# Linear attention and a token/channel mixer on one core: v of the first head group by the plain queue, and another order for batch 1

## The chip, the core and the metric

The kernel runs on one core of a Trainium2 chip. Its engines are TensorE (PE in the profile; PEld is its weight load), VectorE (DVE), ScalarE (ACT), GpSimd (POOL) and SyncE (SP). Each engine works its own queue of instructions in order and they meet by semaphores. Transfers between the chip's memory (HBM) and the core's memory are issued on the queue of SP (hardware-made descriptors, no change of type) or of POOL (software-made descriptors, which can turn fp32 into bf16 under way), and all of them run on the same 16 DMA engines. Matmuls write to PSUM, which has eight banks here.

The metric is the device time of one execution in microseconds (us). A run's span, by the hardware profiler, is from the first instruction to the last; the time is a little longer.

## The reference

Eight batches, eight heads, 576 positions, head size 64; the attention output of one batch is a matrix of 576 x 512, which then goes through a mixer.

```python
phi = lambda x: np.where(x > 0, x, np.exp(x) - 1.0) + 1.0
q_p, k_p = phi(q), phi(k)
kv  = einsum('bhsd,bhse->bhde', k_p, v)
z   = sum(k_p, axis=2)
x   = einsum('bhsd,bhde->bhse', q_p, kv) / (einsum('bhsd,bhd->bhs', q_p, z) + 1e-6)
x   = x as (batch, 576, 512)
u   = x + (relu(x^T @ w_tok1) @ w_tok2)^T      # w_tok1 576 x 256, w_tok2 256 x 576
out = u + relu(u @ w_ch1) @ w_ch2              # w_ch1 512 x 1536, w_ch2 1536 x 512
```

All inputs and the output are fp32; matmuls are in bf16 with fp32 sums.

## The kernel before

The order of all instructions is written by hand; nothing is scheduled by a planner. Each batch's 576 positions are cut into four tiles of 128 (`R = 4`) and a tail of 64; two batches share the tail's 128 rows. The heads of a batch are handled in two groups of four (`c` or `g` = 0, 1).

The steps of a batch, by the names in the code:

- `phi`: e = exp(x) on ScalarE (L125), y = max(x + 1, 1) on VectorE (L131), min(e, y) on VectorE (L139), into `kp` or `qp`. `phi_exp`, `phi_add`, `phi_end` are these three parts; `fe`, `fa`, `fm` place them one by one for batch 1.
- `vcast`: v from fp32 to bf16 (L150), into `vs`, which has a column of ones behind each head's 64 columns.
- `kv`: 36 small matmuls kp^T @ vs (L168); the column of ones gives the sum of kp. Two ScalarE copies (L174) put the result into `kvbd`.
- `qtr`: nine transposes of qp on TensorE (L179), copied out to `qT` (L186). From batch 2 on it is a DMA transpose (`qtr_dma`).
- `nd`: numerator and denominator, qT @ kvbd (L209), then on VectorE den + eps (L218), reciprocal (L220) and the product into x (L221).
- `mm1`, `mm2`: the token mixer (L247 / L258 and L270 / L306, L309); u = x + h. For batch 1 these run in halves of the columns (`mm1_half`, `mm2_half`); the tail is `mm2(1, [R])`, which takes a bank of the pool of four banks (`ps_big`), while for the other batches it lies in the pool of two double banks (`ps_sm`).
- `utr`: u transposed to uT (L325, copy L328), later by DMA.
- `mm3`: uT @ w_ch1, twelve blocks `mc` of four 512-column matmuls (L493), relu to bf16 on ScalarE (L500) or, for two of them, VectorE (L497).
- `mm4`: cr @ w_ch2 (L519); `mm4_end` adds u on VectorE (L536) and sends the rows out.

Steady state: for each batch, a list `big` of blocks of TensorE work (mm3 and mm4) is run through, and a list `fill` says behind which block each step of the next batch stands (`run`). An entry `at(8, vcast, 1, 0)` stands behind block 8. Since every engine's queue is in order, the place in this list is the place in each queue that the step touches.

For batch 0 and 1 the list has 24 blocks: 0 to 2 the second halves of mm3's first three `mc`, 3 to 11 mm3 (`mc` 3 to 11), 12 to 21 `m4_0(kc)`, in which all four row tiles of mm4 get the share of one `kc`, and 22 and 23 `m4_end` (the last two `kc` for row tiles 0, 1 and then 2, 3). So from block 12 to the end mm4's four sums `held[0]` to `held[3]` occupy all four banks of `ps_big`, until `mm4_end(0, t)` has read them.

The start, batch 0, is written out by itself (lines 583 to 706): `e_first`, `r_first`, `p_first` are phi's parts; `kv_first`, `ksum_mm`, `den_mm`, `num_mm` and so on are the steps above in another cut. Here v is loaded by POOL's queue as bf16 into `v0` (`load_v0`, L113, a part of the memory of `cr[1]`), which has no column of ones; so the sum of kp is made by nine extra matmuls (`ksum_mm`, L357) and copied by `ksum_put` (L362). `warm` issues fp32 matmuls on zeros whose result nobody reads.

A gate is a wait put by hand in front of a transfer (`after(ins, other)`): it is issued only when `other` has landed. Before the change q of group 1 waits for k of group 0 (`k_in`), the second v load for the first (`v_in`), batch 1's k of group 0 for the first quarter of w_ch1 (`c_in[0]`) and k of group 1 for its last (`c_in[3]`), the second quarter of w_ch2 for v of batch 1, group 0, and batch 2's q for the second quarter of w_ch2 (`c2_in[1]`). A gated load holds all that stands behind it in its queue.

Of the kernel before, what the change touches and what calls it, by code (L numbers as in the profile page):

```python
# [18 lines left out]
def kernel(  # L19
# [20 lines left out]
    nc = tc.nc  # L40

    B, H, S, D = q.shape
# [3 lines left out]
    R = 4  # L46
# [10 lines left out]
    D1 = D + 1  # L57
# [7 lines left out]
    def const(name, shape, dt=BF16):  # L65
        return consts.tile(shape, dt, name=name, tag=name)
# [36 lines left out]
    def after(ins, other):  # L103
        if other is not None:
            tc.add_manual_dep(ins.ins, other.ins.name, sync_dep, reason="order of transfers")
        return ins

    def load(nm, n, c, gate=None):
        src_ = src[nm][n].rearrange("(j a) (p t) d -> (a p) j (t d)", a=2, t=T)
        js = slice(2 * c, 2 * c + 2)  # L110
        return after(nc.sync.dma_start(out=raw[nm, n % 2][:, js], in_=src_[:, js]), gate)

    def load_v0(c, gate=None):  # L113
        src_ = v[0].rearrange("(j a) (p t) d -> (a p) j (t d)", a=2, t=T)
# [13 lines left out]
    def phi_add(nm, n, j0, nj):  # L128
        f = raw[nm, n % 2][:, j0:j0 + nj].rearrange("p j f -> p (j f)")
        y = work.tile([128, 2 * TD], BF16, name="y", tag="y")[:, :nj * TD]  # L130
        nc.vector.tensor_scalar(out=y, in0=f, scalar1=1.0, scalar2=1.0, op0=ALU.add, op1=ALU.max)  # L131
        for j in range(nj):
            live["y", nm, j0 + j] = y[:, j * TD:]

    def phi_end(nm, n, j0, nj):
        c, i = divmod(j0, 2)
        dst = (kp if nm == "k" else qp)[:, c, :, i:i + nj]
        e, y = live["e", nm, j0], live["y", nm, j0][:, :nj * TD]
        nc.vector.tensor_tensor(  # L139
            out=dst.transpose([0, 2, 1, 3]), in0=e.rearrange("p (i t d) -> p i t d", i=nj, t=T),  # L140
            in1=y.rearrange("p (i t d) -> p i t d", i=nj, t=T), op=ALU.min)
# [6 lines left out]
    def vcast(n, c, copy=nc.scalar.copy):  # L148
        js = slice(2 * c, 2 * c + 2)
        copy(out=vs[:, js, :, 0:D],  # L150
             in_=raw["v", n % 2][:, js].rearrange("p j (t d) -> p j t d", t=T))

    def bank():
        return ps_big.tile([128, 512], FP32, name="bank", tag="big")
# [195 lines left out]

    def qput_first(c, h, put):
        qtr_put(0, c, TS[h], live["qtr", c][h], put, qT[c])

    def ksum_mm(c):
        ps = live["g", c][:, 0:2]
        for t in range(T):
            nc.tensor.matmul(out=ps, lhsT=kp[:, c, t].rearrange("p i d -> p (i d)"),  # L357
                             rhs=ones, start=(t == 0), stop=(t == T - 1))

    def ksum_put(c, copy):  # L360
        for i in range(2):
            copy(out=kvbd[0][half[i], c, :, (i + 1) * D1 - 1], in_=live["g", c][half[i], 0:2])  # L362

    def kv_first(c):

        ps = live["kv", c]
        for t in range(T):
            for a, i in QUARTERS:
                nc.tensor.matmul(out=ps[a][half[i], i * D:(i + 1) * D], lhsT=kp[half[a], c, t, i],
                                 rhs=v0[half[a], 2 * c + i, t],  # L370
                                 start=(t == 0), stop=(t == T - 1))

    def kv_put(c, copy):
        for i in range(2):
            for a in range(2) if c else [slice(0, 2)]:
                copy(out=kvbd[0][half[i], c, a, i * D1:(i + 1) * D1 - 1],
                     in_=live["kv", c][a][half[i], i * D:(i + 1) * D] if c else
                     live["kv2"][half[i], :, i * D:(i + 1) * D])

    def q_cols(r, a, c):  # L380
        t0 = D * (T * (2 * a + c) + 2 * r)
# [203 lines left out]
    nc.vector.memset(zeros, 0.0)  # L585
    nc.vector.memset(one, 0.0)
    nc.scalar.activation(out=one, in_=one, func=AF.Exp)
    k_in = load("k", 0, 0)
    load("q", 0, 0)
    make_identity(nc, identity)  # L590
    v_in = load_v0(0)
    load("q", 0, 1, k_in)
    load("k", 0, 1)
    nc.vector.memset(ones, 0.0)
    for a in range(2):
        nc.vector.memset(ones[half[a], a:a + 1], 1.0)
# [9 lines left out]
    NB = 4  # L606
# [18 lines left out]
    dve, act, pool = nc.vector.tensor_copy, nc.scalar.copy, nc.gpsimd.tensor_copy  # L625
    c_in = [load_wc1(i) for i in range(3)]
# [1 line left out]
        w2_put(kt, t0, t1, pool)  # L628
    c_in.append(load_wc1(3))
    nc.gpsimd.dma_start(out=w1t[half[1], 1, :], in_=w1r[:, 2 * R])  # L630
    c2_in = [load_wc2(0)]

    w_ = bank()
    live["g", 0] = bank()
    live["qtr", 0] = [bank16(), bank16()]
    t_ = sm_tile()
    live["kv2"] = t_[:, :, 0:2 * D]
    live["kv", 0] = [t_[:, a, 0:2 * D] for a in range(2)]
    live["last", 0] = t_[:, 0, 256:256 + HG * D]
    t_ = sm_tile().rearrange("p b (r c) -> p b r c", r=2)  # L640
    live["full", 0] = [t_[:, i] for i in range(2)]
    e_first("k", 0)
    r_first("k", 0)
    warm(w_, 3)
    p_first("k", 0)
    ksum_mm(0)
    e_first("q", 0)
    r_first("q", 0)
    warm(w_, 1, 256)
    kv_first(0)  # L650
    ksum_put(0, act)
    kv_put(0, act)
    p_first("q", 0)
    qtr_first(0)
    qput_first(0, 0, dve)
    qput_first(0, 1, act)
    warm(w_, 1, 256)
    e_first("q", 1)
    r_first("q", 1)
    den_mm(0)  # L660
    num_mm(0)
    den_first(0)
    warm(w_, 1, 256)
    live["qtr", 1] = [bank16(), bank16()]
    live["g", 1] = bank()
    p_first("q", 1)
    e_first("k", 1)
    r_first("k", 1)
    qtr_first(1)
    warm(live["g", 1], 1, 256)  # L670
    p_first("k", 1)
# [35 lines left out]

    for c in range(2):
        for nm in "kqv":
            landed[nm + "1", c] = load(nm, 1, c, c_in[3 * c] if nm == "k" else None)  # L710
    c2_in += [after(load_wc2(i), landed["v1", 0] if i == 1 else None) for i in range(1, NB)]
    for nm in "qkv":
        for c in range(2):
            load(nm, 2, c, c2_in[1] if nm == "q" and c == 0 else None)
# [50 lines left out]
    def fe(s, nm, c):  # L765
        fill.append((s, lambda: phi_exp(nm, 1, 2 * c, 2)))

    def fa(s, nm, c):
        fill.append((s, lambda: phi_add(nm, 1, 2 * c, 2)))

    def fm(s, nm, c):
        fill.append((s, lambda: phi_end(nm, 1, 2 * c, 2)))

    def at(s, fn, *args):
        fill.append((s, lambda: fn(*args)))

    fe(2, "k", 0)
    fa(2, "k", 0)
    fm(3, "k", 0)
    fe(5, "q", 0)  # L780
    fa(5, "q", 0)
    fm(6, "q", 0)
    at(8, qtr, 1, 0, dve)
    at(8, vcast, 1, 0)
    at(10, kv, 1, [0])
    at(11, nd, 1, 0, [0, 1])
    fe(11, "k", 1)
    fa(11, "k", 1)
    at(12, nd, 1, 0, [2, 3])
    fe(12, "q", 1)  # L790
    at(13, nd, 1, 0, [R])
    fm(13, "k", 1)
    fa(13, "q", 1)
    fm(14, "q", 1)
    at(14, vcast, 1, 1)
    at(15, mm1_half, 1, 0)
    at(16, kv, 1, [1])
    at(17, qtr, 1, 1, act)
    at(18, mm2_half, 1, 0)
    at(18, nd, 1, 1, [0, 1])  # L800
    at(19, nd, 1, 1, [2, 3])
    at(20, nd, 1, 1, [R])
    at(20, phi, "q", 2, 0)
    at(20, phi, "q", 2, 1)
    at(21, utr, 1, [0])
    at(21, mm1_half, 1, 1)
    at(22, qtr_dma, 2)
    at(22, load_all, 3, "qkv")
    at(22, mm4_end, 0, 0)
    at(22, mm4_end, 0, 1)  # L810
    at(22, mm2_half, 1, 1)
    at(23, mm2, 1, [R])
    at(23, mm4_end, 0, 2)
    at(23, utr, 1, [1])
    at(23, mm4_end, 0, 3)
    run(big, sorted(fill, key=lambda e: e[0]))

# [69 lines left out]
```

## Time and profile before

| | |
|---|---|
| time, median of 13 runs | 265.39 us (264.68 to 266.55) |
| the profiled execution | 265.11 us, span 263.3 us |
| first matmul of mm1_first (L430) | 16.63 us |
| first matmul of mm3 (L493) | 23.26 us |
| block 3 (mm3, mc 3) | 27.19 us |
| block 12 (m4_0(0), L519) | 36.21 us, with the first nd ahead of it |
| batch 1's mm3 begins | 54.95 us |
| landings: k_raw, q_raw of group 0 | 4.55 and 5.95 us |
| landings: v0 first and second part | 8.2 and 14.7 us |
| landings: q_raw, k_raw of group 1 | 10.46 and 11.9 us |
| landing of wc1's first and last quarter | 19.88 and 29.19 us |
| landing of wc2's first and second quarter | 32.9 and 39.28 us |

The times of instructions are starts on the span's clock. The landings follow from the time of issue and the time to landing of each transfer, or from the end of the wait of the instruction that needed it. From some 57 us to the end TensorE has no hole to speak of: what it does there is the same work in each pair of batches.

### The profile page before, as it was taken

The page shows a single profiled execution, that of the slowest core. Times are in us where ns is not written, and L with a number is a line of the kernel's source. Part 1 is how long each engine was busy: PE and PEld are TensorE (multiplying, and loading weights), DVE is VectorE, ACT ScalarE, POOL GpSimd, SP SyncE. Part 2 cuts the span into 40 slices and gives each one's busy share as a digit, 9 for nine tenths or more (in the row PEclk, how much of TensorE's full clock was granted, in tenths as well). Part 3 has the DMA queues.
Part 4 walks back from the last instruction along what each step waited for, and adds up shares of the span by engine and source line. Part 5 has one row for each costly group of instructions (what it writes and reads, how often), then busy time and mean ns, then how long its engine had stood idle before and what let it go on. Part 6 is the DMA issues. An engine that isn't in the chain of part 4 may idle for free.

```text
span 263.3 us, 5086 instructions
## 1 busy us (share of the span) xinstructions
PE 254.2 (97%) x2080; PEld 132.8 (50%) x2080; DVE 143.8 (55%) x285; ACT 133.9 (51%) x212; POOL 32.1 (12%) x57
## 2 busy tenths in 40 slices
PE   7789999999999999999999999999999999999994
PEld 2565456644744454445554554445554554444642
DVE  4675753976867385848564285828564272520122
ACT  4663794659662358425871368325870363027300
POOL 3752120030001300030001300030001300000000
PEclk9979999999999999999999999999999999999999
DMA  7999999879829990699999980761064500740043
GB/s 210 254 190 271 293 280 290 317 133 316 341 65 162 313 369 4 137 231 364 406 319 218 329 338 1 164 146 42 0 137 114 123 0 2 149 110 0 2 99 100
DMA packets 50087, 48.34 MB, mean 184 GB/s; under 512 B 30288, under 2 KB 35536, under 8 KB 50064
## 3 DMA queue, kind: packets, MB, share of 16 engines
q1 hardware_dynamic: 41904, 35.53, 44.6%
q0 software_dynamic: 7440, 11.44, 21.4%
q10 hardware_dynamic: 720, 1.05, 1.2%
q8 instruction: 16, 0.26, 0.4%
q14 instruction: 7, 0.06, 0.1%
HBM read 35.85 MB, written 9.44 MB: 172 GB/s over the span
## 4 chain that ended last, share of the span: by engine, by line
PE 86%; DMA 6%; DVE 5%; ACT 1%; issue 1%; DVEq 0%
PE c_ps L493 32%; PE h_ps L519 30%; PE a_ps L247 5%; PE c_ps L507 4%; PE h_ps L270 4%; PE nd_ps L209 3%; DMA uT<-u 2%; DMA q_raw<-in_q_dram 2%; PE kv_ps L168 2%; DMA k_raw<-in_k_dram 1%; PE bank L430 1%; PE h_ps L556 1%; DVE y L131 1%; DVE qp L139 1%; DVE o_sb L536 1%; DVE x L221 1%
## 5 line engine op out<-in xcount | busy, mean ns | idle before, releaser
L500 ACT ACTIVATE cr<-c_ps 128x512 bf16<-128x512 f32 x92 | 54.0, 599 | 78.3 <-PE c_ps L493 78.3
L493 PE MATMUL c_ps<-uT,wc 128*128 128x512 bf16 x384 | 91.9, 379 | 0.3 <-DMA uT<-u 0.2
L519 PE MATMUL h_ps<-wc,cr 128*128 128x512 bf16 x372 | 84.9, 379 | 0.0
L519 PEld LDWEIGHTS <-cr 128*128 128x128 bf16 x372 | 35.6, 98 | 41.0 <-issue 1.2
L493 PEld LDWEIGHTS <-wc 128*128 128x128 bf16 x384 | 35.5, 98 | 36.8 <-issue 2.2
L536 DVE TENSOR_TENSOR o_sb<-h_ps,u 128x512 f32<-128x512 f32 x31 | 21.1, 689 | 24.2 <-PE h_ps L519 24.1
L541 POOL DMA_DIRECT2D out_dram<-o_sb x24 | 14.5, 607 | 152.1 <-DVE o_sb L536 152.1
L221 DVE TENSOR_TENSOR x<-nd_ps,den 128x512 bf16<-128x512 f32 (+1 forms) x42 | 25.3, 603 | 1.4
L125 ACT ACTIVATE e<-k_raw 128x1152 bf16<-128x1152 f32 x16 | 18.7, 1169 | 2.6 <-DMA k_raw<-in_k_dram 2.6
L139 DVE TENSOR_TENSOR qp<-e,y 128x1152 bf16<-128x1152 bf16 x16 | 12.1, 759 | 14.0 <-ACT e L125 13.3
L282 DVE TENSOR_TENSOR u<-h_ps,x 128x1024 bf16<-128x1024 f32 x12 | 14.7, 1222 | 9.2 <-PE h_ps L270 9.2
L125 ACT ACTIVATE e<-q_raw 128x1152 bf16<-128x1152 f32 x16 | 18.4, 1159 | 1.0 <-DMA q_raw<-in_q_dram 0.8
L218 DVE TENSOR_SCALAR den<-nd_ps 128x8 f32<-128x8 f32 (+1 forms) x42 | 6.9, 163 | 21.1 <-PE nd_ps L209 20.5
L139 DVE TENSOR_TENSOR kp<-e,y 128x1152 bf16<-128x1152 bf16 x16 | 12.1, 758 | 8.2 <-ACT e L125 7.3
L209 PEld LDWEIGHTS <-qT 128*128 128x128 bf16 x140 | 11.4, 98 | 9.4 <-issue 0.4
L209 PE MATMUL nd_ps<-kvbd,qT 128*128 128x130 bf16 x140 | 15.1, 223 | 0.2 <-ACT u L312 0.2
L150 ACT CAST vs<-v_raw 128x1152 bf16<-128x1152 f32 x13 | 15.0, 1156 | 0.0
L131 DVE TENSOR_SCALAR y<-k_raw 128x1152 bf16<-128x1152 f32 x16 | 12.4, 772 | 2.0 <-DMA k_raw<-in_k_dram 1.9
L546 DVE TENSOR_TENSOR o_sb<-h_ps,ut 128x512 f32<-128x512 f32 x4 | 2.8, 692 | 19.1 <-PE h_ps L519 19.1
L131 DVE TENSOR_SCALAR y<-q_raw 128x1152 bf16<-128x1152 f32 x16 | 12.0, 753 | 0.8 <-DMA q_raw<-in_q_dram 0.8
L247 PE MATMUL a_ps<-x,w 128*128 128x512 bf16 x48 | 12.3, 379 | 0.0
L270 PE MATMUL h_ps<-ar,w2p 128*128 128x512 bf16 x48 | 12.3, 379 | 0.0
(107 smaller groups left out, 206.4 us busy)
## 6 DMA issues: line engine op xcount, KB each, us to landing
k_raw<-in_k_dram SPq DMA_DIRECT2D x16, 576.0 KB, 9.2
q_raw<-in_q_dram SPq DMA_DIRECT2D x16, 576.0 KB, 6.6
v_raw<-in_v_dram SPq DMA_DIRECT2D x14, 576.0 KB, 11.4
out_dram<-o_sb POOLq DMA_DIRECT2D x24, 256.0 KB, 5.1
wc<-in_moe_w_ch_dram POOLq DMA_DIRECT2D x8, 384.0 KB, 9.1
out_dram<-o_sb SPq DMA_DIRECT2D x9, 128.0 KB, 2.3
out_dram<-o_sb ACTq DMA_DIRECT2D x7, 128.0 KB, 2.6
out_dram<-o_sb POOLq DMA_DIRECT2D x6, 128.0 KB, 5.7
```

The costliest lines, as they stand in the source:

```text
L125: nc.scalar.activation(out=e, in_=f, func=AF.Exp)
L131: nc.vector.tensor_scalar(out=y, in0=f, scalar1=1.0, scalar2=1.0, op0=ALU.add, op1=ALU.max)
L139: nc.vector.tensor_tensor(out=dst.transpose([0, 2, 1, 3]), in0=e.rearrange("p (i t d) -> p i t d", i=nj, t=T), in1=y.rearrange("p (i t d) ...
L150: copy(out=vs[:, js, :, 0:D], in_=raw["v", n % 2][:, js].rearrange("p j (t d) -> p j t d", t=T))
L209: nc.tensor.matmul(out=o[:, a], lhsT=qT[b][:, t0:t0 + 128], rhs=kvbd[b][:, c, a], start=True, stop=True)
L221: nc.vector.tensor_tensor(out=x[b][:, rs[0]:rs[0] + m, HG * D * g:HG * D * (g + 1)].rearrange("p r (h d) -> p r h d", h=HG), in0=v_[:, :, ...
L247: nc.tensor.matmul(out=ps[:, mt], lhsT=w1t[:, b, ms] if r == R else w1[:, r, ms], rhs=x[b][:, r, :], start=(r == 0), stop=(r == R))
L270: nc.tensor.matmul(out=ps[:, i], lhsT=w2v(kt, r, b), rhs=ar[b][:, kt, :], start=(kt == 0), stop=(kt == NT - 1 and not add))
L493: nc.tensor.matmul(out=ps, lhsT=wc1[:, kj, 128 * mc:128 * mc + 128], rhs=uT[b][:, :, kj], start=(kj == 0), stop=(kj == NDM - 1))
L500: nc.scalar.activation(out=cr[b][:, mc, :], in_=ps, func=AF.Relu)
L519: nc.tensor.matmul(out=ps, lhsT=crt[:, kc, :] if t == 8 else cr[b][:, kc, 128 * r:128 * r + 128], rhs=wc2[:, kc, :], start=(kc == 0), stop ...
L536: nc.vector.tensor_tensor(out=o, in0=ps, in1=u[b][:, r, :], op=ALU.add)
```

## The change

Five things change.

1. v of batch 0, group 0 is loaded as fp32 on SP's queue into `raw["v", 0]`, as k and q are, in the order k, q, v, q of group 1, k of group 1. No gate stands between them. VectorE casts it to bf16 (`vcast(0, 0, dve)`), and `kv_first(0)` uses `vs` with its column of ones, so group 0 needs no `ksum_mm`, `ksum_put`. Group 1's v is loaded by POOL as before, gated on group 0's v.
2. In the start, group 0's order becomes: phi of k and of q, transposes of q, cast of v, one of the two copies of the transposes, kv, its copies, the other copy. The warm matmuls are placed otherwise (four at the beginning in place of three, two behind `den_first(0)`, none ahead of kv). In group 1 phi's last part for q stands behind the first two parts for k.
3. Batch 1's six loads go out behind one another on SP's queue; only the first has a gate.
4. The first quarter of w_ch2 waits for q of batch 1, group 0; the second for k of batch 1, group 1.
5. Batch 1's steps, and those of batch 2's q, stand at other places among the 24 blocks.

```diff
     def kv_first(c):
-        ps = live["kv", c]
+        m = D if c else D1
         for t in range(T):
             for a, i in QUARTERS:
-                nc.tensor.matmul(out=ps[a][half[i], i * D:(i + 1) * D], lhsT=kp[half[a], c, t, i],
-                                 rhs=v0[half[a], 2 * c + i, t],
+                nc.tensor.matmul(out=live["kv", c][a][half[i], i * m:(i + 1) * m],
+                                 lhsT=kp[half[a], c, t, i],
+                                 rhs=(v0 if c else vs)[half[a], 2 * c + i, t],
...
-    k_in = load("k", 0, 0)
+    load("k", 0, 0)
     load("q", 0, 0)
+    v_in = load("v", 0, 0)
+    load("q", 0, 1)
+    load("k", 0, 1)
     make_identity(nc, identity)
-    v_in = load_v0(0)
-    load("q", 0, 1, k_in)
-    load("k", 0, 1)
...
-    c2_in = [load_wc2(0)]
+    c2_in = []
...
-    warm(w_, 3)
+    warm(w_, 4)
     p_first("k", 0)
-    ksum_mm(0)
     e_first("q", 0)
     r_first("q", 0)
-    warm(w_, 1, 256)
-    kv_first(0)
-    ksum_put(0, act)
-    kv_put(0, act)
     p_first("q", 0)
     qtr_first(0)
+    vcast(0, 0, dve)
+    qput_first(0, 1, act)
+    kv_first(0)
+    kv_put(0, act)
     qput_first(0, 0, dve)
-    qput_first(0, 1, act)
...
-    warm(w_, 1, 256)
+    warm(w_, 2, 256)
...
-    p_first("q", 1)
     e_first("k", 1)
     r_first("k", 1)
+    p_first("q", 1)
...
-            landed[nm + "1", c] = load(nm, 1, c, c_in[3 * c] if nm == "k" else None)
-    c2_in += [after(load_wc2(i), landed["v1", 0] if i == 1 else None) for i in range(1, NB)]
+            landed[nm, c] = load(nm, 1, c, c_in[0] if nm == "k" and c == 0 else None)
+    c2_in += [after(load_wc2(i), {0: landed["q", 0], 1: landed["k", 1]}.get(i)) for i in range(NB)]
```

The places in the list `fill`, behind which block each step stands:

| step | before | after |
|---|---|---|
| k, group 0: exp and add, then min | 2, 3 | 5, 6 |
| q, group 0: exp and add, then min | 5, 6 | 8, 9 |
| cast of v, transposes of q, group 0 | 8, 8 | 10, 11 |
| kv, group 0 | 10 | 11 |
| nd, group 0 (rows 0-1, 2-3, tail) | 11, 12, 13 | 12, 13, 14 |
| k, group 1: add, exp, min | 11, 11, 13 | 11, 12, 14 |
| q, group 1: exp, add, min | 12, 13, 14 | 13, 14, 14 |
| cast of v, group 1 | 14 | 14 |
| mm1_half, group 0's columns | 15 | 14 |
| kv, group 1 | 16 | 14 |
| mm2_half, group 0's columns | 18 | 15 |
| transposes of q, group 1 | 17 | 16 |
| utr, first half | 21 | 16 |
| nd, group 1 | 18, 19, 20 | 17, 18, 19 |
| phi of batch 2's q, groups 0 and 1 | 20, 20, ahead of mm1_half | 20 (behind mm1_half), 21 (behind mm2_half) |
| mm1_half, group 1's columns | 21 | 20 |
| mm2_half, group 1's columns | 22 | 21 |
| mm4_end of row tiles 0 and 1 | 22, ahead of mm2_half | 22 |
| utr, second half | 23 | 22 |
| mm2(1, [R]) | 23 | 22 |

More of the change, by code (lines that the diff above doesn't have):

```diff
@@ L374, in kv_put @@
         for i in range(2):
-            for a in range(2) if c else [slice(0, 2)]:
+            if c == 0:
+                at = slice(i * D1, (i + 1) * D1)
+                copy(out=kvbd[0][half[i], 0, :, at], in_=live["kv2"][half[i], :, at])
+            for a in range(2 * c):
                 copy(out=kvbd[0][half[i], c, a, i * D1:(i + 1) * D1 - 1],
-                     in_=live["kv", c][a][half[i], i * D:(i + 1) * D] if c else
-                     live["kv2"][half[i], :, i * D:(i + 1) * D])
+                     in_=live["kv", c][a][half[i], i * D:(i + 1) * D])
     def q_cols(r, a, c):
@@ L636 @@
     t_ = sm_tile()
-    live["kv2"] = t_[:, :, 0:2 * D]
-    live["kv", 0] = [t_[:, a, 0:2 * D] for a in range(2)]
+    live["kv2"] = t_[:, :, 0:2 * D1]
+    live["kv", 0] = [t_[:, a, 0:2 * D1] for a in range(2)]
     live["last", 0] = t_[:, 0, 256:256 + HG * D]
@@ L775, in at @@
         fill.append((s, lambda: fn(*args)))
[L777 to L787, printed above, removed]
-    fa(11, "k", 1)
[L789 to L793, printed above, removed]
+    fe(5, "k", 0)
+    fa(5, "k", 0)
+    fm(6, "k", 0)
+    fe(8, "q", 0)
+    fa(8, "q", 0)
+    fm(9, "q", 0)
+    at(10, vcast, 1, 0)
+    at(11, qtr, 1, 0, dve)
+    at(11, kv, 1, [0])
+    fa(11, "k", 1)
+    fe(12, "k", 1)
+    at(12, nd, 1, 0, [0, 1])
+    at(13, nd, 1, 0, [2, 3])
+    fe(13, "q", 1)
+    at(14, nd, 1, 0, [R])
+    fm(14, "k", 1)
+    fa(14, "q", 1)
     fm(14, "q", 1)
     at(14, vcast, 1, 1)
[L796 to L802, printed above, removed]
+    at(14, mm1_half, 1, 0)
+    at(14, kv, 1, [1])
+    at(15, mm2_half, 1, 0)
+    at(16, qtr, 1, 1, act)
+    at(16, utr, 1, [0])
+    at(17, nd, 1, 1, [0, 1])
+    at(18, nd, 1, 1, [2, 3])
+    at(19, nd, 1, 1, [R])
+    at(20, mm1_half, 1, 1)
     at(20, phi, "q", 2, 0)
-    at(20, phi, "q", 2, 1)
-    at(21, utr, 1, [0])
-    at(21, mm1_half, 1, 1)
+    at(21, mm2_half, 1, 1)
+    at(21, phi, "q", 2, 1)
+    at(22, mm4_end, 0, 0)
+    at(22, mm4_end, 0, 1)
     at(22, qtr_dma, 2)
     at(22, load_all, 3, "qkv")
[L809 to L812, printed above, removed]
+    at(22, utr, 1, [1])
+    at(22, mm2, 1, [R])
     at(23, mm4_end, 0, 2)
-    at(23, utr, 1, [1])
     at(23, mm4_end, 0, 3)
```

## The prediction

> **What bounds the kernel now.** I read the page first, then busy time by stretches, the chain of waits, the timeline by engine, and the DMA queues in single stretches.
>
> ```profile
> span 263.3 us, 5086 instructions
> PE 254.2 (97%) x2080; PEld 132.8 (50%) x2080; DVE 143.8 (55%) x285; ACT 133.9 (51%) x212; POOL 32.1 (12%) x57
> ```
>
> TensorE is busy for 97% of the span. No matmul of it is removed after the first 16 us (the diff only moves them), so the change acts in two ways: through when the dense stretch of TensorE begins and at what clock, and through new holes in it. The busy time by stretches (columns: stretch in us, its length, each engine's busy time and instructions, granted clock, DMA share, GB/s):
>
> ```profile
> 9.50:12.90 3.40, 2.25 (x32) 1.57 (x31) 2.49 (x6) 2.61 (x3) 3.40 (x6) 1.00 1.05 199
> 12.90:16.30 3.40, 2.40 (x69) 1.78 (x67) 2.87 (x7) 2.49 (x12) 1.55 (x2) 1.00 1.27 179
> 16.30:19.70 3.40, 3.40 (x22) 2.53 (x19) 2.24 (x4) 1.69 (x6) 1.98 (x4) 0.50 1.29 198
> 45.00:56.50 11.50, 11.11 (x85) 6.99 (x83) 9.94 (x20) 6.35 (x8) 1.24 (x2) 1.00 0.73 256
> ```
>
> The sparse start lasts until 16.3; then TensorE is full but has half its clock for 3.4 us; from 45 to 56.5 VectorE is the tight second engine (9.94 of 11.5). The chain of waits in order of time (start, length, what) shows how the start ends:
>
> ```profile
> 13.52 0.77 DVE kp L139
> 14.73 0.52 PE bank L369 x36
> 15.27 0.31 ACT kvbd L376 x2
> 15.86 0.97 PE bank L397 x10
> 16.83 3.65 PE bank L430 x20
> ```
>
> From the timeline (start, length, engine, line, what), the places where batch 1's steps stand today:
>
> ```profile
> 33.01 1.15 ACT L150 CAST vs<-v_raw 128x1152 bf16<-128x1152 f32 x1
> 34.75 0.48 PE L168 MATMUL kv_ps<-vs,kp 64*64 64x65 bf16 x36
> 46.44 2.25 ACT L125 ACTIVATE e<-q_raw 128x1152 bf16<-128x1152 f32 x2 [0.21 <-issue]
> 51.20 0.60 ACT L260 ACTIVATE ar<-a_ps 128x512 bf16<-128x512 f32 x1
> 52.66 1.28 DVE L536 TENSOR_TENSOR o_sb<-h_ps,u 128x512 f32<-128x512 f32 x2
> ```
>
> The cast ends 0.6 us ahead of its reader, and batch 2's exponentials are done long before the relu of mm1's second half. Last, the queues from 32.1 to 35 us (packets, MB, share), in which three wc2 loads had been issued on POOL's queue:
>
> ```profile
> q1 hardware_dynamic: 535, 1.16, 103.5%
> q0 software_dynamic: 8, 0.01, 1.4%
> ```
>
> POOL's queue moves nothing while SP's is full.
>
> **The start.** SP's queue alone moved 0.97 MB from 2.3 to 4.9 us, 0.37 MB/us. Five loads of 0.59 MB behind one another then land at about 4.55 (k, as today), 5.9, 7.5 (v), 9.0 (q1) and 10.5 (k1), against 4.55, 5.95, 8.25 (v0), 10.46 and 11.9. Group 0 by rows: qp 7.30 + 0.76 = 8.05 as today; v's cast, 0.75 (the one L150 on VectorE, at 62.4), 8.8; 36 matmuls of kv 0.48, 9.3; two ScalarE copies 0.27 each (L174), 9.9; den_mm 0.6, 10.5; den_first 0.5, 11.0; then on VectorE y of k1 0.76, qp 0.8, kp 0.8, so kp ends at 13.35, against 14.28. The transposes of q1 still end at 13.2. Behind them ScalarE has L186 0.59, two L419 0.53, ksum_put 0.32 and kv_put 0.65, in all 15.3, against 15.82. But v0's second load, on POOL behind v's landing, gets no engine until SP's queue is empty, at about 10.4; today it began to move after 10 too and landed at 14.7 (8.50 + 6.2). I take 14.4: kv of group 1 then ends at 14.9, kv_put at 15.6, and mm1 starts **0.3 earlier**. The weights behind it gain the same 0.3. Bounds: 0 (v's chain as long as today's) and 1.5 (k1's landing, 11.9 to 10.4). Dropping group 0's ksum (nine matmuls 0.38, two ScalarE copies 0.32) is worth nothing: it ran while TensorE waited 0.75 for v0. The fourth warm matmul lies before qp at 8.05; without that cover it costs 0.85 (5.11 / 6). The 256-column ones moved lie in waits.
>
> **The clock.** mm1_first took 3.65 us for 20 matmuls; at full clock ten of that form take 1.09 (L258), so 2.18: 1.47 is lost to the drop. The stretch ahead of the drop had 2.40 of 3.40 busy, the one ahead of that 2.25 without a drop; what differs is that the first holds 36 small and nine two-column matmuls. After the change the same stretch gains some 0.3 us of mm1 and the number of 128-column matmuls that today fall after 16.3, and the warm ones lie closer together: I take the drop to be gone. Then w2's copies on POOL (17.72 - 0.3 + 1.93 = 19.3) are late for mm2_first's second part, due at 16.3 + 2.2 + 0.44 = 18.95: 0.35 back. **-1.1**; bounds 0 and -1.47.
>
> The Trainium skill speaks differently ("TensorE: Matmul & The Clock Gate", Part 1): half rate comes after an idle window of about 3.4 us, so there should be no drop before or after. The row has one behind a stretch that is 70% busy; by the rule the sum would lack this gain, by the row it has it.
>
> **wc2's first quarter.** It no longer goes out at 20.86 but waits on POOL for q(1,0), which lands at 20.29 - 0.3 + 8.4 = 28.4. By then SP's queue also holds v and the second groups (no gate now): 6 x 0.59 = 3.5 MB, of which 1.2 are moved by 27.3 (58% beside the wc1 quarters, 1.09 MB in 22 to 27); the other 2.3 take 6 us, to 33.2. Today's wc2 load issued at 32.09 landed 7.0 to 7.2 later, at 39.28, some 3.6 after SP's queue had emptied at 35.7: so 36.8. The other bound is 28.4 + 7.0 = 35.4, and far out the longest wc row, 12.0: 40.4. I take 36.1, between the first two. Block 12 (m4_0(0)) wants it: today blocks 3 to 11 start at 27.19; the new start is 25.8, and block 12 is due 9.5 later (below), at 35.3. **+0.8**; bounds 0 and 1.5. The second quarter follows 2 us later, at 38.1 to 38.8, due after block 14: 25.8 + 15 = 40.8, so nothing. POOL has nothing else queued there until the first output.
>
> The skill ("DMA: Bandwidth & Descriptors", Queues, rings and completion order) has each engine go round the queues packet by packet. By that wc2's quarter would move from 29 on and land near 35.2; the two queue rows above show 8 packets against 535. By the rule the wait falls away, by the row it stands.
>
> **Batch 1's order** (zero is the start of block 3; a block of four takes 0.86). Four places, all from the order in which the new instructions stand:
> - ScalarE has e of k at 3.2, e of q at 5.8 (after block 8's relu), two relus of 0.5, the cast at 7.9, done at 9.05. TensorE is through block 11 and the nine transposes at 8.3, and kv waits: **+0.7**. Today's cast stood two blocks ahead of kv.
> - mm1_half(1, 0) stands right behind the last num matmul. Its bank is that of the nd before it, whose three VectorE steps (0.17, 0.20, 0.69, start 0.44 behind) end 1.6 after its first matmul, TensorE 1.2 after: 0.4; then the tail's x another 0.33. **+0.75**.
> - The exponentials of batch 2's q now stand behind mm1_half(1, 1) and its relu. From that matmul's end: relu 0.75, e 1.05, qp 0.8, then u (L314) 0.7, y 0.85, qp 0.7, o_sb 0.7: 5.4 us until bank held[0] is free. mm2(1, [R]) takes that bank (today after block 23, now before it). TensorE has two blocks, mm2_half 1.09 and eight transposes 0.45 until then, 3.3, and waits 0.35 within them for u: **+2.1**. Its cover would be VectorE idle before; it is idle for 2 us then, but its head waits for e.
> - Today's own holes go: 0.39 idle in 45 to 56.5, and three gaps each hide 0.16 of pipelined ends: **-0.9**.
> A further 0.1 for qtr's ScalarE copies ahead of nd. Together +2.75; bounds +1.3 (the middle two halved) and +3.6 (nothing of today's holes goes). Later loads (q of 2 behind wc2's second quarter) come 1 us earlier, batch 3's 2 to 3 us later, with ten blocks until used.
>
> **Sum.** -0.3 - 1.1 + 0.8 + 2.75 = +2.15 on a span of 263.3: 265.4. The profiled run took 265.11, 0.28 under the median, 1.8 outside its span. Median 265.39 + 2.2 = **267.6**; own range 266.4 to 268.8.
>
> **Rivals.**
> - The clock drop stays (the sparse stretch 12.9 to 16.3 is still mostly small matmuls, and full rate was kept with 2.25 busy, lost with 2.40). Block 12 is due at 36.4, so wc2's wait goes too: -0.3 + 2.75 = +2.45, 267.8.
> - The start gives all: k1's 1.5 and the whole 1.47. For it: DVE L139 heads the chain there; against: ScalarE's queue behind unmoved transposes. Weights and batch 1 come 1.2 earlier, wc2 at 34.9 for a block due at 33.7: -3.0 + 1.2 + 2.75 = +0.95, 266.3.
> - Not slower: the new order is hidden. One mechanism: ScalarE and VectorE reach batch 2's q before TensorE wants held[0], as today (e done at 48.7, o_sb at 52.7), and the waits in the stage shrink to today's 0.9. It decides from the point where under 0.6 us of the 2.75 is left: -0.3 - 1.1 + 0.4 = -1.0, 264.4. For it: in the whole of 26 to 45 TensorE never idles today. Against: the two queues go in order, and e stands behind that relu.
>
> **How the numbers follow.** Chances: likeliest 0.44, clock drop stays 0.24, start gives all 0.14, hidden 0.18. A change of 0.2% (0.53 us) is what can be told from none. Faster: 0.16 of the last. Same: the other 0.02 and 0.06 of the third. The rest is slower: 0.16, 0.08, 0.76. The range 264.7 to 269.0 leaves out about 0.12 below and 0.05 above (wc2 near its far bound).
>
> **What would show it.** In the changed kernel's profile: TensorE waits for VectorE at L270 near 1.8 us and for ScalarE at kv near 0.7, SP's queue full until 33 and wc2 landing after 35, PEclk without a 5 near 18, mm1 near 16.3. Wrong if wc2 lands before 34, if no wait over 0.5 stands before L270, or if TensorE's dense stretch begins before 15.5.

## The result, and the profile after

| | |
|---|---|
| time after, median of 11 executions | 269.11 us (267.13 to 271.19) |
| time before, median of 48 executions | 265.37 us (263.96 to 267.25) |
| ratio after / before | 1.013, 95% interval 1.0107 to 1.0153 |
| the profiled execution after | 269.44 us, span 267.6 us |

The changed kernel is slower by 3.7 us. The median of 269.1 is 1.5 us above the predicted 267.6 and 0.1 above the upper end of the range; by the ratio, 1.013 times 265.39, it is 268.8, inside it. Medians are over all executions counted, while the ratios and their intervals leave out executions more than 1.5% above the fastest of their kernel, so a ratio need not be the quotient of two medians.

The page of the changed kernel, three lines: span, busy time by engine, and the granted clock of TensorE in 40 slices.

```profile
span 267.6 us, 5070 instructions
...
PE 253.7 (95%) x2073; PEld 132.6 (50%) x2073; DVE 144.3 (54%) x286; ACT 133.2 (50%) x210; POOL 32.9 (12%) x56
...
PEclk9999999999999999999999999999999999999999
```

TensorE is as busy as before (253.7 us against 254.2) in a span that is 4.3 us longer: what was added is idle time of TensorE. The clock's row has no 7 any more in its third slice.

The changed kernel's busy time by stretches, at the first three of the same places as before (columns: stretch, length, busy time and instructions of PE, PEld, DVE, ACT, POOL, granted clock, DMA share, GB/s):

```profile
9.50:12.90 3.40, 3.04 (x36) 2.28 (x36) 2.79 (x6) 2.66 (x5) 3.40 (x5) 1.00 1.05 156
12.90:16.30 3.40, 3.01 (x75) 2.50 (x75) 2.59 (x7) 3.03 (x15) 1.73 (x3) 1.00 1.11 140
16.30:19.70 3.40, 2.83 (x24) 1.91 (x22) 1.96 (x4) 1.46 (x4) 2.36 (x4) 1.00 1.29 197
```

The stretch from 12.9 to 16.3 has 3.01 us of TensorE against 2.40, and the one behind it runs at 1.00 instead of 0.50. So the start did improve: the first matmul of mm1_first begins at 15.44 (16.63 before), mm3 at 21.69 (23.26), block 3 at 25.55 (27.19). In this profile 1.64 us are won there and more than lost later.

What TensorE waits for in the changed kernel (us in total, times, longest):

```profile
PE h_ps L521 <- DMA wc<-in_moe_w_ch_dram: 3.4, 1, 3.4
PE bank L270 <- DVE o_sb L538: 1.6, 1, 1.6
...
PE bank L442 <- POOL w2p L466: 0.5, 2, 0.3
PE kv_ps L168 <- ACT vs L150: 0.4, 1, 0.4
PE c_ps L495 <- DMA wc<-in_moe_w_ch_dram: 0.3, 1, 0.3
PE a_ps L258 <- DVE x L221: 0.2, 1, 0.2
```

L521 is mm4 (L519 before the change), whose first block, block 12, needs w_ch2's first quarter; L270 is mm2(1, [R]). These two are 5.0 us. Block 12 begins at 38.64 (36.21 before) and batch 1's mm3 at 59.87 (54.95).

The changed kernel's chain of waits, in order of time (start, length, what):

```profile
12.36 7.09 DMA wc<-in_moe_w_ch_dram
19.47 0.37 SPq L111
19.88 10.62 DMA q_raw<-in_q_dram
30.54 0.50 issue
31.04 7.56 DMA wc<-in_moe_w_ch_dram
38.64 1.02 PE h_ps L521 x4
...
52.22 1.11 PE a_ps L258 x10
53.37 0.47 issue
53.84 1.17 ACT e L125
55.03 0.76 DVE qp L139
55.79 0.60 DVE u L314
56.39 0.68 DVE y L131
57.16 0.76 DVE qp L139
57.92 0.61 DVE o_sb L538
```

From 12.36 to 38.6 us it is a chain of three transfers, tied by gates: w_ch1's first quarter lets batch 1's loads out at 19.45, q lands at 30.5, and only then does w_ch2's first quarter go out. Between them stand only some tenths for issuing; no engine's computing decides there. The lower part is the second loss: from mm1_half(1, 1) over the exponential and VectorE's four steps to o_sb, which frees the bank.

The queues of the changed kernel from 28 to 35 us (packets, MB, share):

```profile
q1 hardware_dynamic: 978, 2.11, 77.4%
q0 software_dynamic: 245, 0.22, 22.8%
```

w_ch2's quarter (0.39 MB, issued at 31.04) lies in POOL's queue, q0, while SP's queue, q1, moves ten times as much. From 35 to 38.6, with SP's queue nearly empty (0.03 MB), q0 moves 0.56 MB, and the quarter lands.

SP's queue is not all of the 7.6 us from issue to landing, though. In e6 (below) three quarters are issued at 35.46 beside a nearly empty SP queue, and from 35.5 to 36.8 q0 still moves nothing. Here q0 moves more than a few packets from 33.8 on, 2.8 us after the issue; so some 1.4 us of the 7.6 may be put down to SP's queue, which is an estimate from these two profiles. From 33.8 to 38.6 q0 moves 0.73 MB, nearly twice the quarter: the other three quarters, issued from 34.34 on, are among it. Whether they hold the first one up was not tested.

### The profile page after: what moved, and what is told of

It reads as the page before. It is cut to its first block, busy times and chain, and to the rows that moved or that the text cites. A ratio compares the mean times of both kernels' runs of the same rounds, so it can differ in the third digit from the quotient of the medians.

```text
span 267.6 us, 5070 instructions
## 1 busy us (share of the span) xinstructions
PE 253.7 (95%) x2073; PEld 132.6 (50%) x2073; DVE 144.3 (54%) x286; ACT 133.2 (50%) x210; POOL 32.9 (12%) x56
## 3 DMA queue, kind: packets, MB, share of 16 engines
q10 hardware_dynamic: 720, 1.05, 1.3%
## 4 chain that ended last, share of the span: by engine, by line
PE 81%; DMA 12%; DVE 2%; POOL 2%; issue 1%; SPq 0%; ACT 0%; DVEq 0%; POOLq 0%
PE h_ps L521 33%; PE c_ps L495 27%; DMA wc<-in_moe_w_ch_dram 5%; PE a_ps L247 5%; PE c_ps L509 4%; DMA q_raw<-in_q_dram 4%; PE h_ps L270 4%; PE nd_ps L209 3%; DMA v_raw<-in_v_dram 2%; PE kv_ps L168 2%; PE h_ps L558 1%; PE a_ps L258 1%; DVE x L221 1%; POOL w L624 1%; PE h_ps L291 1%
## 5 line engine op out<-in xcount | busy, mean ns | idle before, releaser
L521 PE MATMUL h_ps<-wc,cr 128*128 128x512 bf16 x372 | 85.1, 379 | 3.4 <-DMA wc<-in_moe_w_ch_dram 3.4
L521 PEld LDWEIGHTS <-cr 128*128 128x128 bf16 x372 | 35.7, 98 | 44.4 <-issue 4.6
L282 DVE TENSOR_TENSOR u<-h_ps,x 128x1024 bf16<-128x1024 f32 x12 | 14.7, 1222 | 9.2 <-PE h_ps L270 9.2
L247 PE MATMUL a_ps<-x,w 128*128 128x512 bf16 x48 | 12.3, 379 | 0.0
L270 PE MATMUL h_ps<-ar,w2p 128*128 128x512 bf16 x48 | 12.3, 379 | 0.0
```

Of the source, the lines that this page charges most:

```text
L247: nc.tensor.matmul(out=ps[:, mt], lhsT=w1t[:, b, ms] if r == R else w1[:, r, ms], rhs=x[b][:, r, :], start=(r == 0), stop=(r == R))
L270: nc.tensor.matmul(out=ps[:, i], lhsT=w2v(kt, r, b), rhs=ar[b][:, kt, :], start=(kt == 0), stop=(kt == NT - 1 and not add))
L521: nc.tensor.matmul(out=ps, lhsT=crt[:, kc, :] if t == 8 else cr[b][:, kc, 128 * r:128 * r + 128], rhs=wc2[:, kc, :], start=(kc == 0), stop ...
```

## The experiments

Each measured beside the kernel before. Its medians in the three groups were 265.12 us (e1 to e4), 265.19 (e5 to e8) and 265.56 (e9 to e12).

### e1: the new start alone

The changed kernel's start; batch 1's loads, gates and places as before.

```diff
-    c2_in = []
+    c2_in = [load_wc2(0)]
...
-            landed[nm, c] = load(nm, 1, c, c_in[0] if nm == "k" and c == 0 else None)
-    c2_in += [after(load_wc2(i), {0: landed["q", 0], 1: landed["k", 1]}.get(i)) for i in range(NB)]
+            landed[nm + "1", c] = load(nm, 1, c, c_in[3 * c] if nm == "k" else None)
+    c2_in += [after(load_wc2(i), landed["v1", 0] if i == 1 else None) for i in range(1, NB)]
```

> The changed start (fp32 v on SP's queue, its order, its warm matmuls) with the loads of batch 1, the waits of wc2 and the order of batch 1 as before. Theory (start gains, the rest loses): mm1_first begins near 15.4, block 3 near 25.6, both as in the changed kernel, and the time is 1.6 us under before, near 263.8. Rival (what the start gains is lost again where the weights land, as wc1 and wc2 come no earlier): block 3 earlier, but holes in front of wc1's last quarter or wc2, and 265.4.

Measured: 264.43 us, ratio 0.9972 (0.9946 to 0.9998), between what theory and rival expected. The start is a gain of 0.7 us, less than the 1.6 that block 3 came earlier in the changed kernel's profile. In e1's profile that gain isn't there: v0's second load landed at 14.6 (12.35 in the changed kernel's), mm1_first began at 16.78, no earlier than the 16.63 of before, the clock's drop is back (0.58 from 16.3 to 19.7), and block 3 began at 26.93. This one execution took 265.36 us. And a new wait stands behind it:

```profile
PE h_ps L521 <- DMA wc<-in_moe_w_ch_dram: 0.7, 1, 0.7
```

That is the second quarter of w_ch2, whose gate did not move when the blocks did. In 8 of e1's 10 executions the mean granted clock was 0.997 or more, against 10 of 25 of the kernel before beside it.

### e2: the new order alone

The kernel before with the changed list of places.

> The kernel before with nothing but the new places of batch 1's steps. Theory: the order costs by itself, 0.4 at kv for ScalarE's cast, 0.5 at mm1_half, 0.2 for u at utr and 1.6 at L270 for bank held[0], less the 0.9 of holes that go: 1.8 us over before, near 267.2. Rival (the order is innocent, its waits only follow wc2's late landing): 265.4 within 0.5, and no wait over 0.5 at L270.

Measured: 267.04 us, ratio 1.0054 (1.0018 to 1.0091). In its profile L270 waits 1.6 us for o_sb, kv 0.5 us for the cast. The order costs by itself, with the old start and without any wait for w_ch2: the rival in which it is hidden falls.

### e3: w_ch2's first quarter without its gate

The changed kernel, the quarter issued right behind w_ch1's last as before.

```diff
-    c2_in = []
+    c2_in = [load_wc2(0)]
...
-    c2_in += [after(load_wc2(i), {0: landed["q", 0], 1: landed["k", 1]}.get(i)) for i in range(NB)]
+    c2_in += [after(load_wc2(i), {1: landed["k", 1]}.get(i)) for i in range(1, NB)]
```

> The changed kernel, but wc2's first quarter goes out on POOL's queue without a wait, as before; all six loads of batch 1 still stand in SP's queue at once. If the wait for q is the cause of the 3.4 us in front of block 12, the quarter lands near 35 and the time falls by some 3 us, to 266. If SP's full queue is the cause, the quarter still lands near 38 and the time stays within 1 us of 269.

Measured: 266.59 us, ratio 1.0045 (1.0016 to 1.0074). POOL issues the quarter at 19.91 and no wait for it is left; block 12 begins at 34.50 instead of 38.64. The one gate is worth 269.11 - 266.59 = 2.5 us (2.3 by the ratios).

### e4: batch 1's second k gated, so that SP's queue holds fewer loads

```diff
-            landed[nm, c] = load(nm, 1, c, c_in[0] if nm == "k" and c == 0 else None)
-    c2_in += [after(load_wc2(i), {0: landed["q", 0], 1: landed["k", 1]}.get(i)) for i in range(NB)]
+            landed[nm, c] = load(nm, 1, c, c_in[3 * c] if nm == "k" else None)
+    c2_in += [after(load_wc2(i), {0: landed["q", 0], 1: landed["v", 0]}.get(i)) for i in range(NB)]
```

> The changed kernel, but k of batch 1's second group waits for wc1's last quarter again, so that SP's queue holds three loads and not six; wc2's first quarter still waits for q of batch 1, its second for v. If SP's full queue is the cause, q lands near 28.5, SP's queue is empty near 31 and the quarter lands near 35: 3 us less, 266. If the wait for q alone is the cause, it lands 7 us behind q all the same, near 36 to 38, and the time falls by 1 us at most.

Measured: 270.27 us over four executions, ratio 1.0176 (1.0133 to 1.0219). q still landed only at 29.6, 9.6 us after its issue, the quarter was issued at 30.14 and landed at 37.4: the wait stays, 2.35 us. So the loss doesn't need the three loads whose gate was gone, and it isn't they that make q late. But e4 did not empty SP's queue: the gate opened at 27.57, ahead of the quarter, and from 30.14 to 34 q1 moved 1.44 MB, q0 0.01. Whether the wait for q alone or SP's queue behind it makes the quarter late is thus not separated by e4. e3 shows that the gate is what costs. The stretches around the wait showed something that nobody had asked for:

```profile
36.00:37.40 1.40, 0.00 (x1) 0.00 (x0) 0.00 (x0) 1.40 (x2) 0.00 (x0) 1.00 1.23 206
37.40:40.00 2.60, 2.38 (x9) 1.22 (x10) 0.23 (x2) 1.52 (x2) 0.00 (x0) 0.50 1.24 204
40.00:42.00 2.00, 2.00 (x12) 0.97 (x11) 1.30 (x5) 0.00 (x0) 0.00 (x0) 0.79 1.24 212
```

As soon as TensorE goes on, its clock is 0.50: 2.38 us of work at a half and 2.00 at 0.79 lose 1.2 + 0.4 = 1.6 us. The hole is paid a second time.

The same in e3's profile, behind the 1.62 us at L270:

```profile
48.40:51.80 3.40, 3.40 (x26) 2.32 (x24) 1.31 (x3) 2.58 (x4) 0.00 (x0) 1.00 1.03 406
51.80:55.20 3.40, 1.58 (x12) 0.78 (x11) 3.21 (x6) 1.62 (x2) 0.00 (x0) 0.96 0.06 21
55.20:58.60 3.40, 3.18 (x9) 1.31 (x9) 2.62 (x4) 0.00 (x0) 2.10 (x4) 0.54 0.85 166
```

A stretch with 1.58 of 3.40 us of work is followed by one at 0.54. In the changed kernel's own profiled execution neither hole brought a drop; it comes in some executions only.

### e5 and e6: which of the moved steps makes L270 wait

Both start from e3. e5 moves mm2(1, [R]) back behind block 23; e6 moves phi of batch 2's q back ahead of mm1_half(1, 1).

```diff
-    at(22, mm2, 1, [R])
+    at(23, mm2, 1, [R])
```

```diff
-    at(20, mm1_half, 1, 1)
     at(20, phi, "q", 2, 0)
+    at(20, phi, "q", 2, 1)
+    at(20, mm1_half, 1, 1)
     at(21, mm2_half, 1, 1)
-    at(21, phi, "q", 2, 1)
```

> The changed kernel with w_ch2's first quarter ungated (the earlier run e3, 266.59 us), and mm2(1, [R]) alone moved back behind block 23. Theory (the sum held[0], read by VectorE's o_sb, comes free 1.6 us after TensorE wants it, because batch 2's exponentials stand behind mm1_half(1, 1)'s relu): only the 0.86 us of block 23's four matmuls move in front of the wait, so L270 still waits, some 0.7 to 0.8 us, and the time falls by about 0.8, to 265.8. Rival (the place of mm2(1, [R]) ahead of block 23 is by itself the cause): the wait goes altogether, 265.0. Second rival (VectorE's late queue holds back all that follows it, the banks of batch 1's mm3 too): the wait only changes its reader, 266.6.

> The same base (266.59 us), and phi of batch 2's q, both groups, moved back ahead of mm1_half(1, 1), as in the kernel before; mm2(1, [R]) stays ahead of block 23. Theory (the late exponentials hold up VectorE's queue): VectorE reaches o_sb about 2 us earlier, L270's wait of 1.6 us falls under 0.4, the time to 265.1 to 265.4; the relu of mm1_half(1, 1) may come later behind the exponentials and mm2_half(1, 1) wait 0.2 to 0.5 for it. Rival (the place of mm2(1, [R]) is the cause): L270 keeps 1.2 us or more, 266.3 to 266.6.

Measured: e5 265.74 us, ratio 1.0015 (0.9998 to 1.0031); L270 still waits 0.8 us, as its theory had it. e6 263.64 us over four executions, ratio 0.9942 (0.9926 to 0.9958), lower than the 265.1 to 265.4 expected; the wait is gone altogether. That is 3 us under e3, more than the wait of 1.6 us; a drop like the one behind the hole in e3's profile would fit the rest, but how much of it that is was not measured. The timeline of e6 (start, length, engine, line, what) shows the order that matters:

```profile
49.77 0.58 ACT L260 ACTIVATE ar<-a_ps 128x512 bf16<-128x512 f32 x1
...
50.88 0.76 DVE L139 TENSOR_TENSOR qp<-e,y 128x1152 bf16<-128x1152 bf16 x1
51.60 0.69 DVE L314 TENSOR_TENSOR u<-h_ps,x 128x512 bf16<-128x512 f32 x1
52.21 1.28 DVE L538 TENSOR_TENSOR o_sb<-h_ps,u 128x512 f32<-128x512 f32 x2
...
52.94 0.59 PE L270 MATMUL bank<-ar,w2p 128*128 128x512 bf16 x2
```

VectorE is through both qp of batch 2 before u and o_sb are wanted, and L270 follows the transposes without a gap. The changed kernel's lines at the same place:

```profile
53.35 0.60 ACT L260 ACTIVATE ar<-a_ps 128x512 bf16<-128x512 f32 x1 [3.60 <-PE a_ps L258]
53.84 1.16 ACT L125 ACTIVATE e<-q_raw 128x1152 bf16<-128x1152 f32 x1
...
55.03 0.76 DVE L139 TENSOR_TENSOR qp<-e,y 128x1152 bf16<-128x1152 bf16 x1 [2.08 <-ACT e L125]
...
57.16 0.76 DVE L139 TENSOR_TENSOR qp<-e,y 128x1152 bf16<-128x1152 bf16 x1
57.84 1.28 DVE L538 TENSOR_TENSOR o_sb<-h_ps,u 128x512 f32<-128x512 f32 x2
58.58 0.59 PE L270 MATMUL bank<-ar,w2p 128*128 128x512 bf16 x2 [1.62 <-DVE o_sb L538]
```

ScalarE stands idle for 3.60 us ahead of the relu with the exponential queued behind it, VectorE then idles 2.08 us for that exponential, and TensorE pays 1.62 us. In e6 the two exponentials lie in ScalarE's idle time.

### e7: e1 with its last wait taken away

The gate of w_ch2's second quarter on batch 1's q instead of its v.

```diff
-    c2_in += [after(load_wc2(i), landed["v1", 0] if i == 1 else None) for i in range(1, NB)]
+    c2_in += [after(load_wc2(i), landed["q1", 0] if i == 1 else None) for i in range(1, NB)]
```

> The kernel with the new start alone (the earlier run e1, 264.43 us, in whose profile L521 waits 0.7 us for w_ch2's second quarter), and the gate of that quarter moved from v of batch 1, group 0, to its q, which lands some 1.5 us earlier. Theory (what is left of the start's gain is spent on this wait, because the weights' gates did not move with the start): the wait goes, 263.8, ratio to the kernel before near 0.995. Rival (the quarter then shares the engines with batch 1's v and the cast waits for v instead): no change, 264.4, with a new wait before kv.

Measured: 265.39 us, ratio 1.0012 (0.9979 to 1.0045): no gain, the executions spread from 263.99 to 268.49. In its profiled execution the wait had changed its place, much as the rival said, though in size far from it. At 268.25 us this is one of its longest executions, so the profile says what can happen, not what the median holds:

```profile
42.79 1.15 ACT L150 CAST vs<-v_raw 128x1152 bf16<-128x1152 f32 x1 [1.69 <-DMA v_raw<-in_v_dram]
44.00 0.48 PE L168 MATMUL kv_ps<-vs,kp 64*64 64x65 bf16 x36 [2.79 <-ACT vs L150]
```

kv of the second group waits for the cast of v, and the cast for v itself. Three quarters of w_ch2 went out on POOL's queue at 28.90, ahead of the second group's loads on SP's (29.78 on), and from 35 to 40 us the two queues move nearly equal numbers of packets (packets, MB, share):

```profile
q1 hardware_dynamic: 471, 1.01, 58.7%
q0 software_dynamic: 469, 0.46, 54.6%
```

In e11 (below) it is the other way round: the quarter goes out at 27.88, behind six loads of SP's queue, and from 30 to 32 us it moves next to nothing:

```profile
q1 hardware_dynamic: 369, 0.80, 101.8%
q0 software_dynamic: 11, 0.01, 3.3%
```

In these two profiles POOL's loads share the engines with SP's when they are issued ahead of them, and move little while SP's are under way when they are issued behind them. The clock is 0.65 from 44 to 47 us behind e7's hole too.

### e8: e1 without warm matmuls

```diff
-    warm(w_, 4)
...
-    warm(w_, 1, 256)
...
-    warm(w_, 2, 256)
...
-    warm(live["g", 1], 1, 256)
```

> The kernel with the new start alone (264.43 us; mean granted clock 0.997 or more in 8 of 10 executions, the kernel before in 10 of 25), and all four groups of warm matmuls left out; their results are read by nothing. Theory of the prediction (TensorE's clock drops to half behind a stretch that is too sparse, and the warm matmuls fill it): the clock lies under 0.997 in most executions, a 5 stands in the clock's row between 6 and 20 us, and the time rises by 1 to 2, to 265.5 to 266.5. Rival (the drop comes by the execution, whatever TensorE does): about as many full-clock executions as with them, 264.4 or a little less.

Measured: 265.16 us, ratio 1.0000 (0.9987 to 1.0013), 0.7 above e1 (the two intervals just overlap). The clock's row doesn't show why: it has no 5, and all 10 executions have a mean granted clock of 0.997 or more. Its timeline does:

```profile
12.79 1.14 PE L179 MATMUL bank<-identity,qp 128*128 128x128 bf16 x9 [0.80 <-DVE qp L139]
...
16.82 1.06 PE L432 MATMUL bank<-x,w 128*128 128x256 bf16 x4
...
18.95 1.05 PE L432 MATMUL bank<-x,w 128*128 128x256 bf16 x8
```

Nine transposes take 1.14 us, where the changed kernel's take 0.68, and four matmuls of 256 columns 1.06, where it takes 0.60 for four in a row (L432 at 16.18). From 18.95 eight take 1.05. TensorE is at half its pace from its first instruction at 8.08 until 18.95, though the row says 1.00. So a full clock in that row means only that no drop was recorded, and the count of executions says nothing of this kernel. The theory's price (265.5 to 266.5) was too high by 0.3 at least, its sign right: with the warm matmuls TensorE has its full pace from the first transposes on. That is not the drop behind a sparse stretch that the theory spoke of; here the pace was never up.

### e9 to e12: putting it together

e9 is e6 with batch 1's first cast of v one block earlier; e10 is e2 with phi of batch 2's q moved back as in e6; e11 is the changed kernel with that same move and nothing else; e12 is e6 once more.

```diff
-    at(10, vcast, 1, 0)
+    at(9, vcast, 1, 0)
```

> The changed kernel with w_ch2's first quarter ungated and phi of batch 2's q ahead of mm1_half(1, 1) (the earlier run e6, 263.64 us over four executions), and batch 1's cast of v, group 0, one block earlier (behind block 9). Theory (every one of the remaining waits is a place in ScalarE's queue): kv's wait of 0.5 us goes, 263.1 to 263.3, ratio to the kernel before near 0.993. Rival (v lands only at 32.3 us, so the cast waits for it and the relus behind it come late): no change or up to 0.5 us longer.

> The kernel before with the changed places of batch 1's steps (the earlier run e2, 267.04 us), and phi of batch 2's q back ahead of mm1_half(1, 1). Theory (of the new order only that one step costs; the rest is within a few tenths): L270's wait goes and the time falls by 1.6 to 2.9, to 264.2 to 265.4, no longer above the kernel before (265.2). Rival (the order costs at other places too, kv and mm1_half among them, and e6 was fast because of the start): 266 or more.

> The changed kernel as it is (269.11 us), and phi of batch 2's q back ahead of mm1_half(1, 1), nothing else. Theory (the wait for w_ch2 at block 12 and the late exponentials are two separate losses): L270's wait goes, L521's 3.4 us for w_ch2 stays, 266.2 to 267.3. Rival (the wait at block 12 already moves ScalarE and VectorE relative to TensorE, so the one hides the other): the sum of the two waits stays near 5, 268.5 or more.

> The earlier run e6 once more, for a firmer number: 263.3 to 264.2 with a clock of 0.997 or more in most executions; where the clock lies under 0.995, about 1 us more. If the theory holds it is faster than the kernel before by 0.3 to 0.7%.

| | us | ratio to before (95%) | executions with clock 0.997 or more |
|---|---|---|---|
| e9 | 263.62 | 0.9932 (0.9908 to 0.9955) | 11 of 11 |
| e10 | 265.61 | 0.9997 (0.9968 to 1.0025) | 3 of 10 |
| e11 | 266.40 | 1.0045 (1.0013 to 1.0077) | 4 of 10 |
| e12 | 263.93 | 0.9943 (0.9916 to 0.9970) | 11 of 12 |
| before, beside them | 265.56 | | 14 of 34 |

e10: with that one step put back the new order costs nothing that can be told, though 265.61 lies 0.2 above the range expected. e11: the step is worth 269.11 - 266.40 = 2.7 us in the changed kernel (2.3 by the ratios), and the wait for w_ch2 stays, so the two losses are separate. In e11's profile that wait is 1.35 us, not 3.4: POOL issues the quarter at 27.88, as q had landed 3 us earlier than in the changed kernel's profile.

```profile
34.11 0.48 PE L168 MATMUL kv_ps<-vs,kp 64*64 64x65 bf16 x36 [0.54 <-ACT vs L150]
35.95 1.02 PE L521 MATMUL h_ps<-wc,cr 128*128 128x512 bf16 x3 [1.35 <-DMA wc<-in_moe_w_ch_dram]
```

e9: kv's wait of 0.5 is gone from its profile, but 263.62 against e12's 263.93 can't be told apart. e6, e9 and e12 are faster than both kernels: by 0.6 to 0.7% than before, and by 5 us than the changed kernel.

## Why the prediction was right in its sign and short in its size

**The start.** Predicted 0.3 us earlier at mm1, measured 1.2 in the profile. Two terms were off there. v0's second load was taken to land at 14.4, since the load of before had needed until 14.7; it landed at 12.35. And ScalarE's four steps, put at 15.3 by the rows of before, ended at 14.87: the transposes were through at 12.95, not 13.2, and the steps overlap by 0.2. But the landing is not a size that one profile fixes: in the ten profiles with the new start and its warm matmuls v0 landed between 12.3 and 14.6 and mm1 began between 15.31 and 16.78. The changed kernel's profile is near the early end, e1's at the late one, where 14.4 was right. That SP's full queue keeps v0 out, as the prediction has it, isn't shown: from 7.7 to 10.4 POOL's queue moved 0.05 MB against SP's 0.81, but the load was issued only at 7.75 and moved its first packets at 9.6; of these 1.85 us e6's rows show some 1.35 without SP's traffic. k1's landing at 10.4 and v's at 7.5 were as worked out.

**The clock.** Predicted -1.1. The drop at 16.3 to 19.7 is indeed gone from the profile, and 0.5 us of waits for POOL's copies of w2 came back, near the 0.35 taken. What the step left out is that the drop is not a constant of a kernel: of the kernel before 34 of the 85 executions in the three groups have a mean clock of 0.997 or more, and by the median they were 1.0, 0.1 and 1.0 us shorter than the others of their group. The median of before thus holds only a part of the 1.47. And the kernels with the new start and no hole over 0.8 us behind it (e5, e6, e9, e12) are at full clock in 36 of 37 executions (e1, whose longest hole there is 0.7 us, in 8 of 10), while the changed kernel is in 5 of 12. That the new holes bring the drop back later is what e3's and e4's profiles show; of the changed kernel no execution with a drop was profiled. The sum had no such term. As to the Trainium skill ("TensorE: Matmul & The Clock Gate", Part 1): e8 agrees with its about 3.4 us of sustained work until full rate (dense from 15.79, full pace at 18.95); its idle window of about 3.4 us ahead of half rate differs from e3 and e4, where holes of 1.6 and 2.35 us sufficed, and the measurement decides.

**wc2's first quarter.** Predicted +0.8, measured 3.4 in the profiled execution, 2.35 in e4's and 1.35 in e11's; by the median the gate is worth 2.5 (e3). The wait itself is as predicted: the gate holds the quarter until q has landed, and block 12 waits for it. What was short are the terms of the sum, each taken from one execution:

| | predicted | e11 | e4 | after |
|---|---|---|---|---|
| q lands | 28.4 | 27.34 | 29.59 | 30.50 |
| from there to the quarter's landing | 7.7 | 8.56 | 7.77 | 8.10 |
| quarter lands | 36.1 | 35.90 | 37.36 | 38.60 |
| block 12 due | 35.3 | 34.60 | 35.05 | 35.27 |

On the average of the three q lands 0.7 us later than predicted, the quarter another 0.4, and block 12 is due 0.3 earlier; that makes up 1.5 of the 1.6 us by which their waits (2.4 on the average) exceed 0.8. q's landing, which had no range of its own, moves by 3.2 us from one profile to another, the quarter's with it by 2.7, the wait by 2.0. Why q takes 8.2 us in one execution and 10.6 in another was not found; e4 shows that it is not for the three loads behind it. The skill's going round packet by packet ("DMA: Bandwidth & Descriptors", Queues, rings and completion order), by which the prediction's other estimate had the quarter land near 35.2, agrees with e7's rows (471 packets against 469) and not with e11's (11 against 369).

**Batch 1's order.** Predicted +2.75, of it 2.1 for mm2(1, [R]) and u: measured 1.62 + 0.21. (The steps listed there add up to 5.55 us, not 5.4; that alone would make it 2.25.) kv 0.4 for 0.7, mm1_half 0.24 for 0.75. By the medians the order alone is +1.9 (e2), and e10 puts nearly all of it on the one step, as the third place of that list had it, down to the relu with the exponential behind it. The smaller places and the holes taken off (-0.9) came to nothing that can be told together; the +0.65 of the text is at the edge of e10's interval.

**The sum by the runs.** -0.7 (e1) + 1.9 (e2) + 2.5 (after less e3) = +3.7, which is the difference measured; by the ratios it is -0.7 + 1.4 + 2.3 = +3.0 of 3.45, so part of that agreement is luck. The gates taken off batch 1's loads and the moved gate of the second quarter have no run of their own. Against it stood -1.4, +2.75 and +0.8. So the term that was most off is wc2's first quarter, sized by single landings; it was short by 1.7 and the start's gain by 0.7 too large, and the order, put 0.85 too high, hid about a third of that.

**The rivals.** Not slower because the new order is hidden: refuted by e2, and the price set for it, under 0.6 us, is what e10 reaches only with the one step put back. The clock drop stays: not in the profile, but 7 of the 12 executions have a mean clock under 0.997; where in them it falls was not seen. The start gives all: nearest in what mm1 gained (1.2 of its 1.5), and its wait for wc2, 1.2, was still short.

**The signs.** L270 waits 1.62 us for VectorE (near 1.8 was named), kv 0.4 for ScalarE (0.7), the quarter lands after 35, PEclk has no 5 near 18. One of the signs set for being wrong did come: mm1_first begins at 15.44, before 15.5, since the start was faster in that execution than the sum had it.

## What to carry to other kernels

A gate on a transfer is a chain: add up the landings along it (here 7.1 + 10.6 + 7.6 us) with the spread that they have from one execution to the next, because the wait at its end takes most of that spread. A gate also changes what stands ahead of a transfer in the other queue: e7 and e11 show the same kind of load sharing the engines evenly or moving next to nothing. In engines that work in order, don't put work that is ready (here batch 2's exponentials) behind an instruction that waits for another engine; moving two calls of one step by a block was worth 2.3 to 2.7 us, more than the whole new start. And a hole in TensorE's dense work may be paid twice, so a change that gains time ahead should be checked for the first hole that it opens behind.

## What the runs showed that was not expected

- A hole of 1.62 us (e3), 2.35 us (e4) or 2.8 us (e7) in dense work was followed by some 3.4 us at half clock in those profiled executions; in the changed kernel's, holes of 1.62 and 3.37 us were not.
- The row of the granted clock can say 1.00 while TensorE works at half its pace: e8's transposes took 1.14 us for nine against 0.68. The pace of a known group has to be looked at beside it.
- Leaving out all warm matmuls cost only 0.7 us in e8, although TensorE was at half its pace for the first 11 us of its work: in its profile TensorE still waits there for VectorE (0.80 us) and ScalarE (0.64 and 0.45).
- From one profile to the next, with the same code up to that place, a landing moves by 2 to 3 us (v0 from 12.3 to 14.6, q of batch 1 from 27.3 to 30.5). A single profile is one draw.
